# All loads of an attention opening issued at once, its value products grouped by tile shape over two banks, its weights later

## The chip, the cores and the metric

The kernel runs on one core of a Trainium2 chip. The metric is the device time of one execution in microseconds (us), the median of several runs of the same built program. Instructions run on five engines: TensorE (PE, with its weight loads shown apart as PEld), VectorE (DVE), ScalarE (ACT), GpSimd (POOL) and SyncE (SP), which issues the DMAs here. Matmuls write PSUM, which has eight banks of 2 KB in each partition; ACT and DVE read it from there.

## The reference

Retention attention without softmax, then a feed-forward layer with a softplus between its two matrices:

```python
scores = scale * np.matmul(q, k.transpose(0, 1, 3, 2))      # 8 batches, 8 heads, 576 x 576, head size 64
ret = scores * Dmat[None, :, :, :]                          # gamma_h ** (i - j) for i >= j, else 0
x = np.matmul(ret, v)                                       # -> 4608 tokens x 512
h = x @ w_in                                                # 512 x 2048
g = np.maximum(h, 0.0) + np.log1p(np.exp(-np.abs(h)))
return (g @ w_out).astype(np.float32)                       # 2048 x 512
```

All inputs and the output are float32.

## The kernel before

**Tiles.** The 4608 tokens are cut into 36 chunks of 128 (`C`), and four chunks make a unit of 512 tokens (nine units). The attention is computed chunk by chunk with a running state of 64 x 64 for each head: a chunk's scores within itself, and a cross term from the state of the chunks before it. The feed-forward layer goes by slots: slot `i` takes unit `i // 16` and block `p = i % 16` of 128 hidden columns. `hidden_mm(i)` is 12 matmuls of 128x512 (L380), `logs` (L388 to L390, ACT) and `softplus` (L394, DVE) follow, `softplus_split` writes the tile `g` (L398 ACT, L399 DVE), and `output_mm(i)` is again 12 matmuls (L412), issued one slot later. Each feed-forward operand is split into a high and a low part, so three products stand for one.

**The first nine chunks** go by doubles. Double `m` is chunk `m // 2` with two pairs of heads, 18 doubles in all, from float32 operands that DMA brings as one block of 512 KB each (`load_double`). For one double:
- `scale_next` (L138, POOL) scales its queries, `scale_values` (L154, ACT, four instructions) its values;
- `scores_double` (PE) makes four score products (L162: 64 rows by 128 columns of the array) and, where a later chunk follows, four state products (L167: 128 rows by 64 columns), into two PSUM banks;
- `scores_double_out`: DVE masks the scores (L177, two instructions) and adds up the state (L186, or a copy at L188), POOL scales the state (L190);
- `values_double` (PE) makes four products of values and masked scores (L203: 128 rows by 64 columns) and, from double 2 on, four cross products of the state and the queries (L207: 64 rows by 64 columns) that add to the same sums. Before, the two pairs (`s`) take turns: two L203, two L207, two L203, two L207, all into one bank;
- `values_double_out`: ACT copies the sums into the unit's tile `xt` as the high part (L216) and DVE takes the rest (L217).

**The opening** handles doubles 0 to 8 (`AHEAD` is 9) before the first slot: doubles 0 to 7 are all of unit 0. In iteration `m`, PE gets the scores of double `m` and then the values of double `m - 1` (at `m = 8` the values come first). It also prepares the first weights. A weight piece is 512 KB of a 64-bit float's two halves; `load_weight` brings it, `weight_a` (ACT L444, DVE L446), `weight_b` (DVE L452), `weight_c` (ACT L460) and `weight_d` (DVE L465) turn it into a high and a low part. Pieces `2p` and `2p + 1` belong to block `p`. Three staging buffers (`WBUFS`) hold pieces, so piece `n` is loaded after `weight_d(n - 3)`.

**Slots 0 to 18** run the feed-forward of unit 0 (and the first slots of unit 1). The odd ones of them, 1 to 17, each hold one of doubles 9 to 17 (scores of `m`, values of `m - 1`), with two banks for both; slot 18 holds the values of double 17. Slots 0 to 14 also prepare two weight pieces each. From slot 19 on, other code with smaller loads makes the attention; the change leaves it alone.

**What sets the order.** The order of each engine is the order of the code, which is written out by hand; nothing is scheduled anew. Five matmuls of 128x256 on a constant (`OPENING`, L498) run while the first loads are under way. All loads and weight loads stand in one queue, SP's, in which a load that waits for its buffer holds back those behind it.

Of the kernel before, what the change touches and what calls it, by code (L numbers as in the profile page):

```python
# [7 lines left out]
F32 = mybir.dt.float32  # L8
# [11 lines left out]
P = 128  # L20
# [14 lines left out]
NPLAIN = PCHUNK * NPAIR  # L35
LEAD = NPLAIN - 2 * (NDOUBLE - AHEAD) - 1
PIECE = 512
START_WEIGHTS = 3
OPENING = 5
OPEN = (6 * C + H + NPAIR, 6 * C)  # L40
RAWS = 2
WBUFS = 3
# [17 lines left out]
def retention_softplus_ffn(ctx: ExitStack, tc, opening, first, others, w, dec, vsc, gchp, out):  # L60
# [1 line left out]

    const = ctx.enter_context(tc.tile_pool(name="const", bufs=1))
    wpool = ctx.enter_context(tc.tile_pool(name="wpool", bufs=1))
    xpool = ctx.enter_context(tc.tile_pool(name="xpool", bufs=2))
    att = ctx.enter_context(tc.tile_pool(name="att", bufs=2))
    moe = ctx.enter_context(tc.tile_pool(name="moe", bufs=2))

# [3 lines left out]
    ps_h = ctx.enter_context(tc.tile_pool(name="ps_h", bufs=2, space=PSUM, side="right"))  # L72


    plain_pools, weight_pools = ExitStack(), ExitStack()
# [23 lines left out]

    def x_tile(u):  # L100
        if u not in xts:
            xts[u] = xpool.tile([P, 2, NKT, T], F32R, tag="xt", name=f"xt{u}")
        return xts[u]


# [1 line left out]
    def load_double(m):  # L107

        if m == 0:
            at = 0  # L110
            for x in parts:
                nc.sync.dma_start(x, opening[:, at:at + x.shape[1]])
                at += x.shape[1]
            kq, kv = (x[:, 0:4 * C] for x in parts)
        elif m == 5:
            kq, kv = (moe.tile([P, 4 * C], F32, tag="ab", name="raw_ab") for _ in range(2))
            for i, x in enumerate((kq, kv)):
                nc.sync.dma_start(x, first[m - 1][:, 4 * C * i:4 * C * (i + 1)])
# [74 lines left out]
    def values_double(m, bank):  # L193
# [17 lines left out]
    def values_double_out(m):  # L211
# [272 lines left out]

    next_double = [6]

    def load_next():
        if next_double[0] < NDOUBLE:
# [1 line left out]
            next_double[0] += 1  # L490

    def bank():
        return ps_att.tile([P, 4 * C], F32, tag="bank", name="bank")


    idle = ps_h.tile([P, T], F32, tag="h", name="idle")
    for n in range(OPENING):
        nc.tensor.matmul(idle[:, 0:2 * C], fill[:, 0:P], fill[:, 0:2 * C], start=True, stop=True)  # L498
    scale_next()
    scale_next()  # L500
    scale_values(0)
    for m in range(AHEAD):
        pair = [ps_y.tile([P, 4 * C], F32, tag=f"y{2 * (m % 2) + h}", name="pair") for h in range(2)]
        if m < AHEAD - 1:
            scores_double(m, pair)
        if m > 0:
            values_double(m - 1, bank())
# [9 lines left out]
        if m in (2, 4, 7):  # L517
            weight_b(m // 2 - 1)
        if m in (3, 5):
            weight_d((m - 3) // 2)  # L520
        if 0 < m < AHEAD - 1:
            values_double_out(m - 1)
        if m in (2, 4, 7):
            weight_c(m // 2 - 1)
        if m in (1, 3, 6):
            weight_a(m // 3)
        scale_next()
    weight_d(START_WEIGHTS - 1)


    SPLIT = NPLAIN - LEAD
    for i in range(NSLOT):
        j = i + LEAD
        if i < SPLIT:
            m = AHEAD + (i - 1) // 2
            if i % 2:
                banks = [bank() for _ in range(2)]
# [3 lines left out]
                values_double_out(m - 1)  # L541
                if i > 1:
                    load_next()
                scale_next()
                if "raw" in later:
                    load_upto(NPLAIN + 1)
            elif i == SPLIT - 1:
                values_double(m, bank())
                values_double_out(m)
            n = START_WEIGHTS + 2 * i  # L550
            weight_a(n)
            weight_cd(n - 1)
# [123 lines left out]
```

## Time and profile before

| what | value |
|---|---|
| median of 3 runs | 954.53 us (954.09 to 954.82) |
| the profiled execution | 954.1 us, of which its span is 952.4 us |
| PE busy | 943.4 us, 99% of the span |
| DVE, ACT, POOL busy | 70%, 71%, 29% of the span |
| granted TensorE clock, mean | 0.999 of full speed |
| all waits of PE for another engine | 4.6 us: 1.5, 1.3, 0.8, 0.8, 0.2 |
| first hidden product starts | 25.81 us |
| DMA in the first 60 us | 14.04 MB, mean 234 GB/s |

The span runs from the first to the last instruction; the profiled execution's own time is 1.7 us more. Times in the rows count from the span's start. The busy time of an engine is its instructions' time; pipelined matmuls overlap, so for PE the starts of consecutive groups tell more than durations. A row of the timeline merges equal neighbours: start, time until the last of them ends, engine, line, operation, output and inputs with shapes, count, and in brackets the idle time before it and what ended that. A float32 matmul shows as two records, so four matmuls are "x8".

### The profile page before, as it was taken

To read this page: it belongs to the slowest core of one execution; us is meant where nothing else is said; L and a number is where in the kernel's file an instruction comes from. 1 tells how busy PE (TensorE), PEld (TensorE's weight loads), DVE (VectorE), ACT (ScalarE), POOL (GpSimd) and SP (SyncE) were. 2 spreads that over 40 slices of the span, in tenths; PEclk is the share of its full clock that TensorE was granted. 3 is DMA by queue.
4 is the path that set the end of the run, shared out by engine and by line. 5 is a ranking of instruction groups with operands and counts; after the bars stand their busy time and mean duration, and the time that the engine had idled before them with its cause. 6 is when DMAs were issued, how large, how long until landed. Compare 5 with 4: busy or idle time off the path is not lost.

```text
span 952.4 us, 14525 instructions
## 1 busy us (share of the span) xinstructions
PE 943.4 (99%) x4946; PEld 788.2 (83%) x4946; DVE 664.5 (70%) x1507; ACT 677.3 (71%) x1449; POOL 279.4 (29%) x497
## 2 busy tenths in 40 slices
PE   8999999999999999999999999999999999999998
PEld 5777778888888888888888888888888888888886
DVE  6788855777877777777777777777777777753222
ACT  6677756777777777777777777777777777764444
POOL 5111112333343332343343343233333333310000
PEclk9999999999999999999999999999999999999999
DMA  8566631212312132212212222213212222201001
GB/s 299 182 200 211 187 137 52 66 52 67 106 56 67 56 105 67 67 51 97 79 52 67 63 99 67 67 50 112 67 50 67 67 95 67 67 1 45 1 1 44
DMA packets 28729, 79.85 MB, mean 84 GB/s; under 512 B 3440, under 2 KB 3440, under 8 KB 28656
## 3 DMA queue, kind: packets, MB, share of 16 engines
q1 hardware_dynamic: 28656, 78.93, 25.7%
q8 instruction: 39, 0.64, 0.3%
q14 instruction: 34, 0.28, 0.1%
HBM read 69.48 MB, written 9.44 MB: 83 GB/s over the span
## 4 chain that ended last, share of the span: by engine, by line
PE 97%; DMA 1%; ACT 1%; DVE 0%; SPq 0%; issue 0%; POOL 0%; ACTq 0%; DVEq 0%
PE h L380 41%; PE y L412 41%; PE os L348 6%; PE sc L266 3%; PE os L275 2%; PE bank L207 1%; PE bank L203 1%; DMA raw_g<-first 1%; PE bank L162 1%; PE pair L162 0%; PE pair L167 0%; PE bank L167 0%; DVE ab L394 0%; DVE g L399 0%; ACT ab L390 0%
## 5 line engine op out<-in xcount | busy, mean ns | idle before, releaser
L380 PE MATMUL h<-xt,w 128*128 128x512 f32 (+1 forms) x1740 | 419.6, 390 | 0.8 <-DVE w L465 0.8
L412 PE MATMUL y<-w,g 128*128 128x512 f32 x1728 | 415.1, 389 | 0.2 <-DVE g L399 0.2
L412 PEld LDWEIGHTS y<-w,g 128*128 128x128 f32 x1728 | 324.2, 188 | 67.9 <-DVE g L399 0.6
L380 PEld LDWEIGHTS h<-xt,w 128*128 128x128 f32 x1740 | 317.3, 188 | 63.0 <-DVE w L465 1.2
L241 POOL TENSOR_TENSOR raw<-raw,dec_sb 128x256 f32<-128x256 f32 x108 | 100.9, 934 | 425.5 <-DMA raw<-others 386.5
L399 DVE TENSOR_TENSOR g<-ab,g 128x512 fp32r<-128x512 f32 (+1 forms) x145 | 103.4, 713 | 87.4 <-ACT g L398 85.6
L394 DVE SCALAR_TENSOR_TENSOR ab<-h,ab 128x512 f32<-128x512 f32 (+1 forms) x145 | 99.7, 688 | 91.2 <-ACT ab L390 88.6
L398 ACT CAST g<-ab 128x512 fp32r<-128x512 f32 (+1 forms) x145 | 89.6, 618 | 99.0 <-DVE ab L394 97.8
L388 ACT ACTIVATE ab<-h 128x512 f32<-128x512 f32 (+1 forms) x145 | 86.3, 595 | 73.7 <-PE h L380 73.6
L390 ACT ACTIVATE ab<-ab 128x512 f32<-128x512 f32 (+1 forms) x145 | 91.3, 629 | 4.7
L389 ACT ACTIVATE ab<-ab 128x512 f32<-128x512 f32 (+1 forms) x145 | 91.3, 629 | 4.6
L255 ACT CAST hl<-raw 128x768 fp32r<-128x768 f32 x108 | 90.9, 841 | 0.0
L285 DVE TENSOR_TENSOR a<-sc,a 128x256 f32<-128x256 f32 x108 | 45.9, 425 | 60.9 <-ACT a L284 60.8
L361 ACT CAST xt<-os 64x128 fp32r<-64x128 f32 x216 | 56.4, 261 | 44.0 <-PE os L275 39.9
L257 DVE TENSOR_TENSOR hl<-raw,hl 128x512 fp32r<-128x512 f32 x108 | 84.7, 785 | 1.5
L348 PE MATMUL os<-ah,hl 128*128 128x256 f32 x324 | 72.7, 285 | 0.0
L365 DVE TENSOR_TENSOR xt<-os,xt 64x128 fp32r<-64x128 f32 x216 | 62.3, 288 | 2.8
L309 POOL TENSOR_TENSOR s<-s,gchp_sb 128x128 f32<-128x128 f32 x96 | 59.4, 618 | 10.5 <-DVE s L308 0.4
L348 PEld LDWEIGHTS os<-ah,hl 128*128 128x128 f32 x324 | 53.3, 191 | 0.1
L286 POOL TENSOR_SCALAR_AFFINE_SELECT a<-a 128x256 f32<-128x256 f32 x108 | 44.2, 410 | 29.6 <-DVE a L285 28.1
L256 DVE TENSOR_TENSOR hl<-raw,hl 64x256 fp32r<-64x256 f32 x108 | 45.9, 425 | 6.7 <-ACT hl L255 3.7
L317 ACT CAST ah<-a 128x256 fp32r<-128x256 f32 x108 | 44.0, 408 | 6.9 <-POOL a L286 3.9
(91 smaller groups left out, 782.5 us busy)
## 6 DMA issues: line engine op xcount, KB each, us to landing
raw<-others SPq DMA_DIRECT2D x108, 384.0 KB, 3.0
wst<-w SPq DMA_DIRECT2D x32, 512.0 KB, 3.7
out<-osb SPq DMA_DIRECT2D x34, 256.0 KB, 2.3
raw_rawp<-first SPq DMA_DIRECT2D x13, 512.0 KB, 4.9
raw_g<-first SPq DMA_DIRECT2D x3, 512.0 KB, 7.6
raw_ab<-first SPq DMA_DIRECT2D x2, 256.0 KB, 8.6
dec_sb<-dec SPq DMA_DIRECT2D x1, 512.0 KB, 3.6
out<-part SPq DMA_DIRECT2D x2, 256.0 KB, 2.4
```

Source lines behind the costliest of these rows:

```text
L241: nc.gpsimd.tensor_mul(r[:, 2:4], r[:, 2:4], later["dec"][:, 2 * pr:2 * pr + 2])
L255: nc.scalar.copy(hl[:, 0:6], r)
L257: nc.vector.tensor_sub(hl[:, 6:10], r[:, 2:6], hl[:, 2:6].bitcast(F32))
L348: nc.tensor.matmul(o[:, :, 0:width], lhs, rhs, start=(n == 0), stop=(n == len(mms) - 1))
L380: nc.tensor.matmul(h, ws[p][:, a, kt * P:(kt + 1) * P], xt[:, b, kt, cols], start=(n == 0), stop=(n == 3 * NKT - 1))
L388: nc.scalar.activation(ab, h, AF.Abs)
L389: nc.scalar.activation(ab, ab, AF.Exp, scale=-1.0)
L390: nc.scalar.activation(ab, ab, AF.Ln, bias=1.0)
L394: nc.vector.scalar_tensor_tensor(ab, h, 0.0, ab, op0=ALU.max, op1=ALU.add)
L398: nc.scalar.copy(g[:, HI], ab)
L399: nc.vector.tensor_sub(g[:, LO], ab, g[:, HI].bitcast(F32))
L412: nc.tensor.matmul(y, g[:, a, at:at + P], ws[p][:, b, PIECE:], start=(p == 0 and n == 0), stop=(p == NF - 1 and n == 2))
```

## The change

1. **Value products.** `values_double` now makes all four L203 products (L202 now) and then all four L207 products (L208 now). The two pairs write two different banks, at columns 384 to 511 of each. `ps_att` becomes one tile of two banks instead of two tiles of one. In the opening the odd iterations use the two `ps_h` banks instead, and there the copy out takes two instructions of 128 columns on ACT and two on DVE. Elsewhere one instruction on each reads both banks. In the odd slots the tile of two banks holds the scores and state products of double `m` too. In the built program ACT's copy there now waits for DVE's state sum, the third of DVE's reads of that tile; before, it waited for the second mask product only.
2. **Loads.** All nine loads of the opening are issued at its start. Doubles 5 to 8 go into four buffers of a new pool `rawx`, whose room is the odd units' `xt` buffer, opened in slot 1 (`xodd`) when these doubles are done; `xpool` keeps one buffer, for the even units. Load 3 now stands ahead of the first weight piece.
3. **Weights.** Pieces 0, 1, 2 are loaded after loads 3, 5, 7 and their steps come one to two iterations later; `weight_b(2)` comes after the opening, and `weight_c(2)`, `weight_d(2)` in slot 0.
4. **Warm-up.** Four matmuls at the start, and one after the scores of double 0, instead of five.

```diff
-OPENING = 5
+VCOLS = slice(3 * C, 4 * C)
+OPENING = (4, 1)
-    xpool = ctx.enter_context(tc.tile_pool(name="xpool", bufs=2))
+    xpool = ctx.enter_context(tc.tile_pool(name="xpool", bufs=1))
-    ps_att = plain_pools.enter_context(tc.tile_pool(name="ps_att", bufs=2, space=PSUM))
+    ps_att = plain_pools.enter_context(tc.tile_pool(name="ps_att", bufs=1, space=PSUM))
-    wst = weight_pools.enter_context(tc.tile_pool(name="wst", bufs=WBUFS, side="right"))
+    wst = weight_pools.enter_context(tc.tile_pool(name="wst", bufs=WBUFS))
+    rawx = load_pools.enter_context(tc.tile_pool(name="rawx", bufs=4, side="right"))
...
-            pool, tag = (moe, "g") if m in (3, 4, 8) else (rawp, "rawp")
+            pool, tag = (moe, "g") if m in (3, 4) else (rawx, "rawx") if 4 < m < AHEAD else (rawp, "rawp")
...
-        o = bank[:, 2 * C:4 * C].rearrange("p (s c) -> p s c", s=2)
+        o = [b[:, VCOLS] for b in banks]
         for s in range(2):
             for h in range(2):
                 rows = slice(h * D, (h + 1) * D)
-                nc.tensor.matmul(o[rows, s], L["v"][:, s, rows], L["a"][:, h, s], start=True,
+                nc.tensor.matmul(o[s][rows], L["v"][:, s, rows], L["a"][:, h, s], start=True,
                                  stop=not n_cross, skip_group_check=True)
-            for h in range(2) if n_cross else ():
-                rows = slice(h * D, (h + 1) * D)
-                nc.tensor.matmul(o[rows, s, 0:n_cross], L["before"][rows, s], L["q"][rows, s, 0:n_cross],
-                                 start=False, stop=True, skip_group_check=True)
+        if n_cross:
+            for s in range(2):
+                for h in range(2):
+                    rows = slice(h * D, (h + 1) * D)
+                    nc.tensor.matmul(o[s][rows, 0:n_cross], L["before"][rows, s], L["q"][rows, s, 0:n_cross],
+                                     start=False, stop=True, skip_group_check=True)
...
-        nc.scalar.copy(xt[:, HI, pr:pr + 2, cols], o)
-        nc.vector.tensor_sub(xt[:, LO, pr:pr + 2, cols], o, xt[:, HI, pr:pr + 2, cols].bitcast(F32))
+        if both is None:
+            parts = [(pr + s, o[s]) for s in range(2)]
+        else:
+            parts = [(slice(pr, pr + 2), both[:, :, VCOLS])]
+        for p, src in parts:
+            nc.scalar.copy(xt[:, HI, p, cols], src)
+        for p, src in parts:
+            nc.vector.tensor_sub(xt[:, LO, p, cols], src, xt[:, HI, p, cols].bitcast(F32))
...
-    for m in range(6):
+    for m in range(AHEAD):
         load_double(m)
-        if m in (2, 5):
-            load_weight(m // 3)
+        if m in (3, 5, 7):
+            load_weight((m - 3) // 2)
...
-        if m in (2, 3, 4, 7, 8):
+        if m in (3, 6):
             load_next()
-        if m in (3, 5, 7):
-            load_weight((m + 1) // 2)
+        if m in (5, 8):
+            load_weight(m // 3 + 2)
...
-    weight_d(START_WEIGHTS - 1)
+    weight_b(START_WEIGHTS - 1)
...
-                banks = [bank() for _ in range(2)]
-                scores_double(m, banks)
-                values_double(m - 1, banks[1])
+                both = bank()
+                scores_double(m, halves(both))
+                values_double(m - 1, halves(both))
+                if "xodd" not in later:
+                    load_pools.close()
+                    later["xodd"] = ctx.enter_context(tc.tile_pool(name="xodd", bufs=1, side="right"))
                 scores_double_out(m)
-                values_double_out(m - 1)
+                values_double_out(m - 1, both)
```

PE in the opening, iterations 4 and 5 (`pair` are score banks, `a_260` the masked scores of double 3, `s_192` the state), before:

```order
L162 MATMUL pair<-raw_g 128x128 x4
L167 MATMUL pair<-raw_g 64x64 x4
L203 MATMUL bank<-a_260,raw_g 64x128 x2
L207 MATMUL bank<-raw_g,s_192 64x128 x2
L203 MATMUL bank<-a_260,raw_g 64x128 x2
L207 MATMUL bank<-raw_g,s_192 64x128 x2
L162 MATMUL pair<-raw_ab 128x128 x4
```

The same place in the changed program:

```order
L165 MATMUL pair<-raw_g 64x64 x4
L202 MATMUL bank<-a_267,raw_g 64x128 x4
L208 MATMUL bank<-raw_g,s_202 64x128 x4
L160 MATMUL pair<-raw_rawx 128x128 x4
L165 MATMUL pair<-raw_rawx 64x64 x4
L202 MATMUL hv<-a_303,raw_g 64x128 x4
L208 MATMUL hv<-raw_g,s_233 64x128 x4
```

The two shapes of the value products follow each other once in a double instead of three times; every second double writes the `ps_h` banks (`hv`).

SP's queue from its start (`part` is double 0, `wst` a weight piece, the others doubles in order), before:

```order
L112 DMA part_93<-opening 128x780
L112 DMA part_94<-opening 128x768
L122 DMA raw_rawp<-first 128x1024 x2
L438 DMA wst<-w 128x1024
L122 DMA raw_g<-first 128x1024 x2
L118 DMA raw_ab<-first 128x512 x2
L438 DMA wst<-w 128x1024
L122 DMA raw_rawp<-first 128x1024 x2
L438 DMA wst<-w 128x1024
```

And in the changed program:

```order
L114 DMA part_96<-opening 128x780
L114 DMA part_97<-opening 128x768
L120 DMA raw_rawp<-first 128x1024 x2
L120 DMA raw_g<-first 128x1024
L446 DMA wst<-w 128x1024
L120 DMA raw_g<-first 128x1024
L120 DMA raw_rawx<-first 128x1024
L446 DMA wst<-w 128x1024
L120 DMA raw_rawx<-first 128x1024 x2
L446 DMA wst<-w 128x1024
L120 DMA raw_rawx<-first 128x1024
```

Load 3 (the first `raw_g`) has moved ahead of weight piece 0, and loads 6 to 8 up from the middle of the opening; none of these rows waits for a buffer any more.

## Rows read from the trace of the kernel before

**Rows 1.** The page's part 1: busy time, share of the span, instructions, by engine.

```profile
PE 943.4 (99%) x4946; PEld 788.2 (83%) x4946; DVE 664.5 (70%) x1507; ACT 677.3 (71%) x1449; POOL 279.4 (29%) x497
```

**Rows 2.** The view of waits, PE, whole span: us in total, times, longest.

```profile
PE pair L162 <- POOL raw_rawp L138: 1.3, 1, 1.3
PE h L380 <- DVE w L465: 0.8, 1, 0.8
PE pair L162 <- POOL raw_g L138: 0.8, 1, 0.8
PE y L412 <- DVE g L399: 0.2, 1, 0.2
```

**Rows 3.** Timeline of the opening, loads and PE: start, us, engine, line, operation.

```profile
1.53 3.92 PE L498 MATMUL idle<-fill 128*128 128x256 f32 x10 [1.53 <-DVE fill L474]
...
6.90 1.06 ACT L154 ACTIVATE raw_rawp<-raw_rawp,part 128x64 f32<-128x64 f32 x4 [0.81 <-DMA raw_rawp<-first]
...
10.00 0.40 POOL L190 TENSOR_TENSOR s<-s,part 128x128 f32<-128x128 f32 x1 [1.04 <-DVE s L188]
...
10.75 1.06 ACT L154 ACTIVATE raw_g<-raw_g,part 128x64 f32<-128x64 f32 x4 [0.41 <-DMA raw_g<-first]
...
11.57 0.71 PE L162 MATMUL pair<-raw_g 64*128 64x128 f32 x8 [0.77 <-POOL raw_g L138]
```

**Rows 4.** Timeline of the opening, PE's value products of doubles 0 and 3.

```profile
8.72 0.61 PE L203 MATMUL bank<-a,part 128*64 128x128 f32 x8
...
9.26 0.72 PE L162 MATMUL pair<-raw_rawp 64*128 64x128 f32 x8
...
14.85 0.39 PE L203 MATMUL bank<-a,raw_g 128*64 128x128 f32 x4
...
15.17 0.44 PE L207 MATMUL bank<-raw_g,s 64*64 64x128 f32 x4
...
15.53 0.44 PE L203 MATMUL bank<-a,raw_g 128*64 128x128 f32 x4
...
15.90 0.44 PE L207 MATMUL bank<-raw_g,s 64*64 64x128 f32 x4
...
16.27 0.71 PE L162 MATMUL pair<-raw_ab 64*128 64x128 f32 x8
```

**Rows 5.** Timeline of slots 0 to 2, PE.

```profile
25.81 3.04 PE L380 MATMUL h<-xt,w 128*128 128x512 f32 x12
...
37.54 3.06 PE L380 MATMUL h<-xt,w 128*128 128x512 f32 x12 [0.79 <-DVE w L465]
...
40.80 3.04 PE L412 MATMUL y<-w,g 128*128 128x512 f32 x12 [0.20 <-DVE g L399]
```

**Rows 6.** Timeline of slot 0, DVE.

```profile
27.42 0.42 DVE L446 TENSOR_SCALAR wst<-wst 128x512 int32<-128x512 uint32 x1
...
27.95 1.04 DVE L452 SCALAR_TENSOR_TENSOR wst<-wst 128x512 int32<-128x512 int32 x1
...
30.90 0.69 DVE L394 SCALAR_TENSOR_TENSOR ab<-h,ab 128x512 f32<-128x512 f32 x1 [1.91 <-ACT ab L390]
```

**Rows 7.** Timeline of slots 5 and 7, PE, first score product of each.

```profile
57.03 0.71 PE L162 MATMUL bank<-raw_rawp 64*128 64x128 f32 x8
...
70.49 0.72 PE L162 MATMUL bank<-raw_rawp 64*128 64x128 f32 x8
```

**Rows 8.** Timeline, DVE, the tile g of slots 1, 3 and 13.

```profile
40.05 0.69 DVE L399 TENSOR_TENSOR g<-ab,g 128x512 fp32r<-128x512 f32 x1
...
53.12 0.68 DVE L399 TENSOR_TENSOR g<-ab,g 128x512 fp32r<-128x512 f32 x1
...
119.97 0.69 DVE L399 TENSOR_TENSOR g<-ab,g 128x512 fp32r<-128x512 f32 x1
```

**Rows 9.** Timeline of slot 5, DVE's state sum and ACT's copy.

```profile
61.27 0.28 DVE L186 TENSOR_TENSOR s<-bank,s 128x128 f32<-128x128 f32 x1
...
61.38 0.37 ACT L216 CAST xt<-bank 128x256 fp32r<-128x256 f32 x1 [1.98 <-DVE a L177]
```

More of the change, by code (lines that the diff above doesn't have):

```diff
@@ L72, in retention_softplus_ffn @@
     ps_h = ctx.enter_context(tc.tile_pool(name="ps_h", bufs=2, space=PSUM, side="right"))
-    plain_pools, weight_pools = ExitStack(), ExitStack()
-    ps_att = plain_pools.enter_context(tc.tile_pool(name="ps_att", bufs=2, space=PSUM))
+    plain_pools, weight_pools, load_pools = ExitStack(), ExitStack(), ExitStack()
+    ps_att = plain_pools.enter_context(tc.tile_pool(name="ps_att", bufs=1, space=PSUM))
     rawp = plain_pools.enter_context(tc.tile_pool(name="rawp", bufs=2))
     pconst = plain_pools.enter_context(tc.tile_pool(name="pconst", bufs=1))
-    wst = weight_pools.enter_context(tc.tile_pool(name="wst", bufs=WBUFS, side="right"))
+    wst = weight_pools.enter_context(tc.tile_pool(name="wst", bufs=WBUFS))
+    rawx = load_pools.enter_context(tc.tile_pool(name="rawx", bufs=4, side="right"))
     later = {}
@@ L101, in x_tile @@
         if u not in xts:
-            xts[u] = xpool.tile([P, 2, NKT, T], F32R, tag="xt", name=f"xt{u}")
+            xts[u] = later.get("xodd" if u % 2 else "", xpool).tile([P, 2, NKT, T], F32R, tag="xt", name=f"xt{u}")
         return xts[u]
@@ L114, in load_double @@
             kq, kv = (x[:, 0:4 * C] for x in parts)
[L115 to L118, printed above, removed]
         else:
-            pool, tag = (moe, "g") if m in (3, 4, 8) else (rawp, "rawp")
+            pool, tag = (moe, "g") if m in (3, 4) else (rawx, "rawx") if 4 < m < AHEAD else (rawp, "rawp")
             r = pool.tile([P, 8 * C], F32, tag=tag, name=f"raw_{tag}")
@@ L191, in scores_double_out, with values_double @@
             states[m % 2] = s
-    def values_double(m, bank):
+    def values_double(m, banks):
         L = live[-1 - m]
@@ L202, in values_double, with values_double_out @@
                 rows = slice(h * D, (h + 1) * D)
-                nc.tensor.matmul(o[rows, s], L["v"][:, s, rows], L["a"][:, h, s], start=True,
+                nc.tensor.matmul(o[s][rows], L["v"][:, s, rows], L["a"][:, h, s], start=True,
                                  stop=not n_cross, skip_group_check=True)
-            for h in range(2) if n_cross else ():
-                rows = slice(h * D, (h + 1) * D)
-                nc.tensor.matmul(o[rows, s, 0:n_cross], L["before"][rows, s], L["q"][rows, s, 0:n_cross],
-                                 start=False, stop=True, skip_group_check=True)
+        if n_cross:
[4 more added lines that the diff above has]
+                                     start=False, stop=True, skip_group_check=True)
         L["o"] = o
-    def values_double_out(m):
+    def values_double_out(m, both=None):
         o = live.pop(-1 - m)["o"]
@@ L483, in retention_softplus_ffn @@
     nc.gpsimd.memset(mask2[0:S % C, S % C:C], 0.0)
-    next_double = [6]
+    next_double = [AHEAD]
     def load_next():
@@ L492, in bank, with halves, warm @@
     def bank():
-        return ps_att.tile([P, 4 * C], F32, tag="bank", name="bank")
+        return ps_att.tile([P, 2, 4 * C], F32, tag="bank", name="bank")
+    def halves(tile):
+        return [tile[:, n] for n in range(2)]
     idle = ps_h.tile([P, T], F32, tag="h", name="idle")
-    for n in range(OPENING):
-        nc.tensor.matmul(idle[:, 0:2 * C], fill[:, 0:P], fill[:, 0:2 * C], start=True, stop=True)
+    def warm(count):
+        for n in range(count):
+            nc.tensor.matmul(idle[:, 0:2 * C], fill[:, 0:P], fill[:, 0:2 * C], start=True, stop=True)
+    warm(OPENING[0])
     scale_next()
@@ L503, in retention_softplus_ffn @@
         pair = [ps_y.tile([P, 4 * C], F32, tag=f"y{2 * (m % 2) + h}", name="pair") for h in range(2)]
+        if m % 2:
+            both, vbanks = None, [ps_h.tile([P, 4 * C], F32, tag="h", name="hv") for _ in range(2)]
+        else:
+            both = bank() if m else None
+            vbanks = m and halves(both)
         if m < AHEAD - 1:
             scores_double(m, pair)
+        if m == 0:
+            warm(OPENING[1])
         if m > 0:
-            values_double(m - 1, bank())
+            values_double(m - 1, vbanks)
         if m == AHEAD - 1:
             scores_double(m, pair)
-            values_double_out(m - 1)
-        if m in (2, 3, 4, 7, 8):
+            values_double_out(m - 1, both)
+        if m in (3, 6):
             load_next()
-        if m in (3, 5, 7):
-            load_weight((m + 1) // 2)
+        if m in (5, 8):
+            load_weight(m // 3 + 2)
         scale_values(m + 1)
         scores_double_out(m)
[L517 to L520, printed above, removed]
+        if m in (3, 6):
+            weight_b(m // 3 - 1)
+        if m in (4, 7):
+            weight_d(m // 3 - 1)
         if 0 < m < AHEAD - 1:
[L522 to L525, printed above, removed]
+            values_double_out(m - 1, both)
+        if m in (3, 6):
+            weight_c(m // 3 - 1)
+        if m in (2, 5, 8):
             weight_a(m // 3)
         scale_next()
-    weight_d(START_WEIGHTS - 1)
+    weight_b(START_WEIGHTS - 1)
     SPLIT = NPLAIN - LEAD
@@ L536, in retention_softplus_ffn @@
             if i % 2:
-                banks = [bank() for _ in range(2)]
-                scores_double(m, banks)
-                values_double(m - 1, banks[1])
+                both = bank()
[4 more added lines that the diff above has]
+                    later["xodd"] = ctx.enter_context(tc.tile_pool(name="xodd", bufs=1, side="right"))
                 scores_double_out(m)
-                values_double_out(m - 1)
+                values_double_out(m - 1, both)
                 if i > 1:
@@ L547, in retention_softplus_ffn @@
             elif i == SPLIT - 1:
-                values_double(m, bank())
-                values_double_out(m)
+                both = bank()
+                values_double(m, halves(both))
+                values_double_out(m, both)
             n = START_WEIGHTS + 2 * i
```

## The prediction, made before the changed kernel ran

> **What bounds the kernel now.** I start with the page's busy times: PE is busy for 99% of the span [rows 1], so a gain has to be less work on PE or one of its few waits. The view of waits names them [rows 2]: besides the wait for the warm-up's constant they sum to 3.1 us, all of it in the first 41 us, and behind that PE never stands. So whatever shortens PE's row of work behind 41 us arrives at the end in full, unless another engine becomes the bound. For that I read the timeline, first PE in the opening [rows 3, 4], then PE, DVE and ACT in the slots [rows 5 to 9]. The reader is to see two things there. PE loses time where the shapes of its products change. And from slot 1 to slot 13 DVE and ACT, which prepare weights there, are nearly as slow as PE: DVE finishes `g` of slot 1 at 40.74 and PE starts to use it at 40.80, having stood for it; `g` of slot 3 ends 13.06 us later, while PE needs 13.46 from one odd slot to the next [rows 5, 7, 8].
>
> **The value products.** Where all four products of one shape stand together they take 0.54 us (8.72 to 9.26). The first two of them take 0.32 where a change of shape follows (14.85 to 15.17), so two more in the same shape cost 0.22. In turns, each further group of two takes 0.36 or 0.37 (15.17 to 15.53, to 15.90, to 16.27). Double 3 takes 1.42 so; grouped it should take 0.54 for the first shape and 0.36 + 0.22 for the second, 1.12 [rows 4]. That is 0.30 less for each double with a cross term: 2 to 17, sixteen. The cross products of doubles 8 and 9 are half as wide, but the cost is the change, so I take 0.30 there too. The second bank has no row of its own: between 0 (a new bank costs as much as a new shape) and 0.30 I take 0.30, since the four score products also alternate between two banks and run at the steady pace.
>
> **The opening.** Everything up to the values of double 1 stays, since it hangs on the first three loads, whose order stays. The shorter warm-up, four products of 3.92 / 5 = 0.78 each, lets double 0 start up to 0.4 us earlier, but double 1 then waits for load 1 as before (1.3 us of waits), so it is worth nothing [rows 2, 3]. Load 3 is next. Load 2, weight piece 0 and load 3 land in the 3.85 us between ACT's first use of load 1 and of load 3, 1.28 each; without piece 0 ahead of it load 3 lands near 9.45 instead of 10.7. But POOL works on double 1's state until 10.40, and from there the scaling and its hand-over to PE take the 0.8 that lie between load 3's use at 10.75 and PE's start at 11.57, so PE starts double 3 at 11.2: 0.37 of the 0.77 us wait [rows 3]. Bounds: 0, if POOL is late, and 0.77. Then come six value groups, doubles 2 to 7, of 0.30: 1.8. Against it stands DVE, which gets more work in a shorter stretch (the odd iterations' copies in two parts, weight steps later); I take 0.1 for the last masked scores coming late, between 0 and 0.5. Sum of the opening: 0.37 + 1.8 - 0.1 = 2.1 us, bounds 1.3 and 2.6; the first hidden product starts near 23.7 instead of 25.81 [rows 5].
>
> Covers in the opening. The loads: at 1.28 each behind load 1 at 6.87, load 4 lands at 12.0 and is scaled at 12.8, PE wants it at 13.25; loads 5 to 8 land at 13.3, 15.8, 17.1, 19.7, PE wants them at 15.3, 17.35, 19.4 and 22.6. Load 4 has the least slack, 0.45; each further us of lateness would be a us lost. On SP, pieces 0 to 2 move behind loads 3, 5 and 7, and loads 9 and 10 and pieces 3 and 4 follow; piece 3 is the twelfth block behind load 1, 6.87 + 12 x 1.28 = 22.2, and is wanted when slot 0 begins. A copy of 128 columns has no row; two of them cost between one and two of the 0.37 us that 256 columns take [rows 9], on ACT and likewise on DVE. The last copy before the first hidden product is a single one, so I price this at nothing beyond the 0.1 above.
>
> **Slots 0 to 2.** DVE gets `weight_a(2)` and `weight_b(2)` into the stretch before slot 0's softplus; it idles 1.91 us there, and the two are 0.42 and at most 1.04 [rows 6], so they are covered, by 0.4 at the worst. From the first hidden product to the output product of slot 1 pass 14.99 us (25.81 to 40.80), of which PE stands 0.99 for DVE [rows 5]: the chain of logs, softplus, weights and `g` sets this stretch, not PE. So double 8's 0.30 is lost here. And the chain grows: ACT's copy, so far released by DVE's second mask product, has to wait for the state sum too. In slot 5 that ends at 61.55, the copy began at 61.38 [rows 9], and ACT works without a pause behind it. That adds 0.2 us. Slots 0 to 2: +0.2, between -0.3 and +0.4.
>
> **Slots 3 to 13**, six pairs of slots. PE's pair falls from 13.46 [rows 7] to 13.16. The chain took 13.06 in the first pair, where PE had just stood for it, and (120.66 - 40.74) / 6 = 13.32 on average, part of which is DVE and ACT waiting for PE [rows 8]. With the copy's 0.2 that is 13.26 to 13.52. I take 13.27, because the first pair is the one in which PE was held by the chain, as it will be in all. So each pair gains 0.19, not 0.30: six give 1.1. Bounds: 1.8 gained, if PE stays the bound, and 0.4 lost, at 13.52.
>
> Here a rule counts against the change. The row shows ACT's copy of value sums standing 1.98 us for a DVE instruction that reads other columns of the same bank [rows 9]. The Trainium skill (PSUM — Partial Sum Buffer, "PSUM bank collisions raise a hardware error") says that two engines must not touch one bank in the same partitions at once, reads against reads included. By that rule a copy that reads both banks has to stand behind all of DVE's reads of both, the state sum among them, and the trace agrees as far as it shows such a wait for the one bank. Without it the pairs would come out at PE's 13.16.
>
> **Slots 14 to 18.** Weight preparation is over at slot 14, and nothing but PE binds: the values of doubles 15, 16 and 17 give 3 x 0.30 = 0.9.
>
> **Sum.** -2.1 + 0.2 - 1.1 - 0.9 = -3.9 us against the profiled execution's 954.1: 950.2. That execution was 0.4 us under the median of the runs, 954.53, so I forecast 950.6 for the median.
>
> **Rivals.** (a) The chain of DVE and ACT binds all the way, at 13.52 for a pair: for it, the average of 13.32 and the new wait; against it, the first pair's 13.06. Then -2.1 + 0.2 + 0.4 - 0.9 = -2.4, 952.1. (b) PE stays the bound: the copy's longer wait falls into time that DVE and ACT have, for instance because POOL's work, earlier by then, disturbs DVE less. Then -2.2 - 1.8 - 0.9 = -4.9, 949.6. (c) The change doesn't do what it says: with two banks the changes of shape cost what they did. Then the 0.37 of load 3 and the copy's 0.2 remain, 954.4; the 0.54 of a group of four speaks against it. (d) Slower: with 13 transfers outstanding the early loads share the engines with the later ones. Eleven blocks, loads 1 to 8 and pieces 0 to 2, at 1.28 would all land near 6.87 + 10 x 1.28 = 19.7, and PE's double 1 would start some 12.8 us late; less the 3.9 gained that is +8.9, 963.4. It decides as soon as load 1 lands more than 3.9 + 1.9 us later than 6.87. Against it: before, ten transfers are outstanding by then and still land one behind the other [rows 3].
>
> **How the numbers follow.** My forecast 0.49, (a) 0.22, (b) 0.20, (c) 0.06, (d) 0.03. A measurement of this kernel tells 0.2%, 1.9 us, from no change. The forecast, (b) and most of (a) are faster by more than that, 0.87; (c) and (a)'s worst are within it, 0.09; (d) and whatever of (c) also loses are slower, 0.04. All gains at their bounds give -2.6 - 0.3 - 1.8 - 0.9 = -5.6, all losses -1.3 + 0.4 + 0.4 - 0.9 = -1.4. With the 0.4 that is 948.9 to 953.1; both ends at once are rare on the upper side, so I cut it to 952.9, and that leaves out about 2 in 10 with (c) and (d).
>
> **What would show it.** First hidden product between 23.2 and 24.5; a value group of 1.12 us; a wait of at most 0.4 for load 3; the output product of slot 1 near 38.9; waits of PE for `g`, some 0.1 us each, in the even slots up to 14, with ACT's copies released by DVE's state sum; no wait of PE behind slot 14. It is wrong if the value group stays above 1.3, if the first hidden product comes after 25, or if an odd pair takes more than 13.5 us.

## The result and the profile after

The changed kernel takes 956.29 us (median of 14 runs, 955.67 to 958.20), the kernel before 954.24 beside it (14 runs): a ratio of 1.0022, with an interval of 1.0015 to 1.0030. It is 2.0 us slower, not 3.9 faster, and lies above the forecast's range. The profiled execution has a span of 954.4 us.

Most of what the prediction named is there all the same. The page's first part and the waits of PE, to be held against [rows 1, 2]:

```profile
span 954.4 us, 14523 instructions
PE 946.1 (99%) x4946; PEld 789.2 (83%) x4946; DVE 662.2 (69%) x1511; ACT 676.3 (71%) x1453; POOL 276.5 (29%) x497
```

```profile
PE h L388 <- DVE w L473: 1.0, 1, 1.0
PE pair L160 <- POOL raw_rawx L136: 0.8, 1, 0.8
PE pair L160 <- POOL raw_rawp L136: 0.2, 1, 0.2
PE y L420 <- DVE g L407: 0.2, 1, 0.2
```

The waits fell from 3.1 to 2.2 us, yet PE is busy for 2.7 us more with the same 4,946 instructions. That is the first sign: the loss is no wait, the same products take longer. Next the opening, of the changed kernel, by the timeline (load 3 is the first `raw_g`, load 6 the second `raw_rawx`), against [rows 3, 4]:

```profile
10.71 0.72 PE L160 MATMUL pair<-raw_g 64*128 64x128 f32 x8
...
13.72 0.61 PE L202 MATMUL bank<-a,raw_g 128*64 128x128 f32 x8
...
14.26 0.65 PE L208 MATMUL bank<-raw_g,s 64*64 64x128 f32 x8
...
14.85 0.72 PE L160 MATMUL pair<-raw_rawx 64*128 64x128 f32 x8
...
16.97 1.06 ACT L152 ACTIVATE raw_rawx<-raw_rawx,part 128x64 f32<-128x64 f32 x4 [1.57 <-DMA raw_rawx<-first]
...
17.80 0.71 PE L160 MATMUL pair<-raw_rawx 64*128 64x128 f32 x8 [0.83 <-POOL raw_rawx L136]
```

A value group takes 1.13 us (13.72 to 14.85) where it took 1.42, and load 3 holds nothing up any more. New is a wait of 0.83 for load 6. The first hidden product and the slots, against [rows 5, 7]:

```profile
24.09 3.06 PE L388 MATMUL h<-xt,w 128*128 128x512 f32 x12
...
38.90 3.02 PE L420 MATMUL y<-w,g 128*128 128x512 f32 x12 [0.18 <-DVE g L407]
...
49.37 3.06 PE L388 MATMUL h<-xt,w 128*128 128x512 f32 x12
52.57 3.06 PE L420 MATMUL y<-w,g 128*128 128x512 f32 x12
55.56 0.72 PE L160 MATMUL bank<-raw_rawp 64*128 64x128 f32 x8
...
68.82 0.72 PE L160 MATMUL bank<-raw_rawp 64*128 64x128 f32 x8
...
82.08 0.72 PE L160 MATMUL bank<-raw_rawp 64*128 64x128 f32 x8
```

A pair of slots takes 13.26 us (55.56 to 68.82 to 82.08) where it took 13.46. The starts of products in the timeline, from here to the end, tell where the time goes:

| product | before | changed | difference |
|---|---|---|---|
| hidden, slot 0 | 25.81 | 24.09 | -1.72 |
| output of slot 1 | 40.80 | 38.90 | -1.90 |
| output of slot 13 | 121.49 | 119.23 | -2.26 |
| hidden, slot 19 (unit 1) | 152.82 | 150.03 | -2.79 |
| hidden, slot 32 (unit 2 begins) | 236.88 | 235.13 | -1.75 |
| slot 48 (unit 3) | 341.36 | 339.61 | -1.75 |
| slot 64 (unit 4) | 444.08 | 443.61 | -0.47 |
| slot 80 (unit 5) | 548.55 | 548.09 | -0.46 |
| slot 96 (unit 6) | 651.28 | 652.09 | +0.81 |
| slot 112 (unit 7) | 755.76 | 756.57 | +0.81 |
| slot 128 (unit 8) | 857.88 | 859.98 | +2.10 |

2.8 us are gained up to slot 19. Then every odd unit loses 1.28 us (1.04 in the thirteen slots of unit 1 from slot 19 on) and no even unit loses anything: 0.080 us for each slot of an odd unit, 64 slots, 5.1 us. Two slots of unit 3, first of the kernel before, then of the changed one:

```profile
417.92 2.91 PE L380 MATMUL h<-xt,w 128*128 128x512 f32 x12
420.66 2.88 PE L412 MATMUL y<-w,g 128*128 128x512 f32 x12
...
424.45 2.91 PE L380 MATMUL h<-xt,w 128*128 128x512 f32 x12
```

```profile
417.13 2.96 PE L388 MATMUL h<-xt,w 128*128 128x512 f32 x12
419.94 2.90 PE L420 MATMUL y<-w,g 128*128 128x512 f32 x12
...
423.75 2.96 PE L388 MATMUL h<-xt,w 128*128 128x512 f32 x12
```

There is no wait in either. Twelve hidden products take 2.81 us from their start to the output's (417.13 to 419.94) where they took 2.74 (417.92 to 420.66). In unit 3 their mean spacing (from start to start) is 233.6 ns in the changed kernel and 229.2 before; in unit 4 it is 228.5 in both. The output products behind them in unit 3 are spaced 228.7 ns instead of 226.6, and 12 x (4.4 + 2.1) ns is the slot's 0.08 us. What differs between odd and even units is the tile `xt` alone: the change gave the odd units' tile another place. As built, the weights start at byte 16576 of each partition, the odd tile before at 164032, now at 212960.

### The profile page after: what moved, and what is told of

It is laid out like the page before. It is cut to its first block, busy times and chain, and to the rows that moved or that the text cites. A ratio compares the mean times of both kernels' runs of the same rounds, so it can differ in the third digit from the quotient of the medians.

```text
span 954.4 us, 14523 instructions
## 1 busy us (share of the span) xinstructions
PE 946.1 (99%) x4946; PEld 789.2 (83%) x4946; DVE 662.2 (69%) x1511; ACT 676.3 (71%) x1453; POOL 276.5 (29%) x497
## 4 chain that ended last, share of the span: by engine, by line
PE 96%; ACT 1%; DVE 1%; DMA 0%; POOL 0%; issue 0%; DVEq 0%; ACTq 0%; POOLq 0%
PE h L388 41%; PE y L420 40%; PE os L356 6%; PE sc L274 3%; PE os L283 2%; PE bank L208 1%; PE pair L160 1%; PE bank L202 1%; PE bank L160 0%; PE idle L511 0%; DMA wst<-w 0%; PE pair L165 0%; DVE a L175 0%; DVE ab L402 0%; DVE g L407 0%; ACT ab L397 0%
```

## The experiments

Each ratio is against the kernel before, measured beside that run on the same chip.

**1. The odd tile moved by 32 bytes.** The pools on the right side grow downward, so a tile of 32 unused bytes ahead of `rawx` moves the odd tile to 212928. Nothing is computed differently. (The buffers of the small loads lie below that tile and move too, but odd and even units use them alike.)

```diff
+    pad = ctx.enter_context(tc.tile_pool(name="pad", bufs=1, side="right"))
+    pad.tile([P, 8], F32, name="pad")
     plain_pools, weight_pools, load_pools = ExitStack(), ExitStack(), ExitStack()
```

> The changed kernel with an unused tile of 32 bytes ahead of the odd units' tile, which then starts at a multiple of 64 bytes (212928) instead of 32 past one (212960). The changed kernel loses 0.080 us in each of the 64 slots of units 1, 3, 5 and 7 and nothing in the even units. Theory A, the start of the tile within 64 bytes: the 64 slots take what they took before the change, so 956.3 - 64 x 0.080 = 951.2 us; the opening and slots 0 to 18 keep their gain of 2.8 us. Rival B, the place of the tile (near the top of SBUF, beside the buffers of the small loads): stays at 956.3.

Measured 951.37 us, ratio 0.9965 [0.9952, 0.9977]. Odd units' slots are again as long as before to the hundredth. Two slots of unit 3:

```profile
415.86 2.91 PE L390 MATMUL h<-xt,w 128*128 128x512 f32 x12
418.61 2.88 PE L422 MATMUL y<-w,g 128*128 128x512 f32 x12
...
422.40 2.91 PE L390 MATMUL h<-xt,w 128*128 128x512 f32 x12
```

So 32 bytes of address are worth about 5 us (4.9 by the two medians), and without that loss the change is 3 us faster than the kernel before.

**2. The odd tile moved by 64 bytes** (the same tile with 16 columns, address 212896).

> The same with 64 bytes: the odd units' tile moves further than in the other run, but starts 32 past a multiple of 64 again (212896). Theory A: 956.3 us, 0.080 us lost in each odd unit's slot. If a mere move mended it, it would come to 951.2 like the other, and A would fall.

Measured 954.78, ratio 1.0004 [0.9995, 1.0013]: odd slots are 0.053 us longer, not 0.080. It loses, as expected, but by a third less; "not a multiple of 64" has no room for two prices.

**3. The kernel before with its odd tile moved by 32 bytes** (the tile in a pool of its own between two unused tiles of 32 bytes; everything allocated behind it on the left side, `g` too, moves by 64).

> The kernel before, with only the odd units' tile moved by 32 bytes (164064 instead of 164032), everything behind it moved by 64. Theory A: each of the 64 slots of units 1, 3, 5 and 7 costs 0.080 us more, 954.2 + 5.1 = 959.3 us. Rival B: the place stays, so 954.2 us.

Measured 969.23, ratio 1.0150 [1.0135, 1.0166], 10 us more than expected. The loss is not in odd units alone. The page's groups of hidden (L385) and output (L417) products, then the same two of the kernel before:

```profile
L417 PE MATMUL y<-w,g 128*128 128x512 f32 x1728 | 426.3, 395 | 0.2 <-DVE g L404 0.2
L385 PE MATMUL h<-xt,w 128*128 128x512 f32 (+1 forms) x1740 | 424.4, 392 | 0.8 <-DVE w L470 0.8
```

```profile
L380 PE MATMUL h<-xt,w 128*128 128x512 f32 (+1 forms) x1740 | 419.6, 390 | 0.8 <-DVE w L465 0.8
L412 PE MATMUL y<-w,g 128*128 128x512 f32 x1728 | 415.1, 389 | 0.2 <-DVE g L399 0.2
```

The output products read `g` as weights and the tile `w` as moving rows, and neither is the odd tile; `g` had moved by 64 bytes, from one multiple of 64 to another, and they became 11.2 us slower. My theory of a multiple of 64 fell here. Every fast pair of tiles had one thing in common: the moving tile and the tile of weights start at the same place within 128 bytes. That gave two new theories for the next three runs: the distance between the two counts, or each must have its own place.

**4, 5 and 6. Distance or place.** 96 unused bytes on the right (odd tile at 212864); the same with 64 unused bytes ahead of everything on the left; and those 64 with the 32 of the first run.

```diff
     gchp_sb = const.tile([P, NPAIR], F32, name="gchp_sb")
+    const.tile([P, 16], F32, name="pad64")
```

> The change with 96 unused bytes ahead of the odd units' tile: it starts at 212864, a multiple of 128, while the weights, the even units' tile, g and hl all stay at addresses that leave 64 when divided by 128. Theory A (a matmul's moving rows must start at a multiple of 64): as with 32 unused bytes, 951.4 us, hidden products of odd units at 229 ns. Theory R (the moving rows and the weights loaded beside them must start at the same place within 128 bytes; the kernel before had all of them at 64): hidden products of odd units some 4 to 5 ns longer, 0.05 to 0.08 us more for each of 64 slots, 954.8 to 956.5. Theory S (each operand by itself must leave 64): as R here.

> As the kernel with the odd units' tile at a multiple of 128, and 64 more unused bytes ahead of everything on the other side, so that weights, both tiles, g and hl all start at multiples of 128. Theory A: 951.4 us. Theory R (the same place within 128 bytes is what counts): 951.4 us, every pitch as before. Theory S (each must leave 64): hidden and output products slow in every unit, 144 slots times some 0.16 us, near 974.

> 64 unused bytes ahead of weights, even units' tile, g and hl, which start at multiples of 128, and the odd units' tile left at 64 within 128 (the 32 byte pad). Theory A: 951.4 us. Theory R: hidden products of the odd units alone 4 to 5 ns longer, 954.8 to 956.5. Theory S: outputs slow in all units and hidden products in the even ones, 144 times 0.08 plus 80 times 0.08, near 969.

Measured, with the distance from the weights to the odd tile within 256 bytes as the programs were built:

| kernel | odd tile less weights | distance | odd slot | us | ratio |
|---|---|---|---|---|---|
| before | 147456 | 0 | 0 | 954.24 | 1 |
| 32 bytes of padding (run 1) | 196352 | 0 | 0.000 | 951.37 | 0.9965 [0.9952, 0.9977] |
| the change | 196384 | 32 | +0.080 | 956.29 | 1.0022 [1.0015, 1.0030] |
| 64 bytes (run 2) | 196320 | 224 | +0.053 | 954.78 | 1.0004 [0.9995, 1.0013] |
| run 4 | 196288 | 192 | +0.080 | 956.09 | 1.0019 [1.0010, 1.0028] |
| run 5 | 196224 | 128 | +0.067 | 955.42 | 1.0014 [1.0005, 1.0024] |
| run 6 | 196288 | 192 | +0.080 | 956.58 | 1.0026 [1.0016, 1.0035] |

Run 6 has the odd tile where run 1 had it and is slow; runs 4 and 6 have neither the weights nor the odd tile at the same address, but the same distance and the same price. So it is the distance. Run 5 was meant to be fast by a period of 128 and is not: the period that fits is 256. A period of 512 does not fit, since the distances of the kernel before and of run 1 differ by 191 x 256 bytes and both are fast.

**7. TensorE alone.** A kernel that leaves out the whole computation and makes stretches of 192 products, in the order of the hidden products, at nine distances. Beside TensorE only one copy of ACT's, 0.6 us, runs at the start of a stretch.

```diff
+    for xt in moving:
+        stretch(weights, xt)
+    stretch(weights, moving[0])
+    stretch(later_weights, moving[1])
+    stretch(later_weights, moving[0])
```

The tiles in `moving` start 0, 32, 64 and so on up to 256 bytes on from the weights, within 256; `later_weights` start 32 bytes on, so that the last but one stretch has both tiles moved by 32 and the last has a distance of 224.

> TensorE by itself: twelve stretches of 192 products (64 or fewer instructions of other engines run only before and after a stretch), each product with 128x128 weights and 512 moving columns in the order of the hidden products. The moving tile starts 0, 32, 64, 96, 128, 160, 192, 224 and 256 bytes past a multiple of 256 from the weights, then 0 again, then 0 with both moved by 32 bytes, then 224 with the weights moved. It leaves the whole computation out. Theory R256 (what counts is the distance between the two tiles that one product reads, within 256 bytes): about 227 ns per product (43.6 us a stretch) at 0, 256 and with both moved, 230 to 234 ns (44.3 to 44.9 us) at all others, as in the odd units of the runs with the tile moved (0.053 to 0.080 us in 12 products). Rival (the other engines' reads and writes collide with TensorE's, and TensorE alone does not care): 227 ns in all twelve.

The page's groups, named by the distance (busy us of a stretch, mean ns of a product's own duration):

```profile
L97 PE MATMUL h<-d_onesixty,weights 128*128 128x512 f32 x192 | 45.1, 396 | 0.0
L97 PE MATMUL h<-d_ninetysix,weights 128*128 128x512 f32 x192 | 45.0, 395 | 0.0
L97 PE MATMUL h<-d_thirtytwo,weights 128*128 128x512 f32 x192 | 45.0, 395 | 0.0
L97 PE MATMUL h<-d_oneninetytwo,weights 128*128 128x512 f32 x192 | 45.0, 394 | 0.0
L97 PE MATMUL h<-d_zero,weights_thirtytwo 128*128 128x512 f32 x192 | 45.0, 396 | 0.0
L97 PE MATMUL h<-d_onetwentyeight,weights 128*128 128x512 f32 x192 | 45.0, 395 | 0.0
L97 PE MATMUL h<-d_twotwentyfour,weights 128*128 128x512 f32 x192 | 45.0, 395 | 0.0
L97 PE MATMUL h<-d_sixtyfour,weights 128*128 128x512 f32 x192 | 44.1, 391 | 0.0
L97 PE MATMUL h<-d_thirtytwo,weights_thirtytwo 128*128 128x512 f32 x192 | 43.7, 389 | 0.0
L97 PE MATMUL h<-d_twofiftysix,weights 128*128 128x512 f32 x192 | 43.7, 389 | 0.0
```

At 256 and with both tiles moved by 32 a stretch takes 43.7 us, at every other distance but one 45.0 or 45.1: 1.3 / 192 = 6.8 ns for each product. Only 64 lies between, 44.1. (The two stretches at 0 stand in one group of 384 and are left out here: beside the first, ACT and DVE were still filling tiles. By the starts of its products the second has the pace of 256.) The granted clock was 1.00 in all eleven stretches behind the first. So no other engine is needed: the rival is out, and what counts is how TensorE's own two tiles lie to each other. How the two reads hinder each other no run here shows. The distance also explains run 3: there the moving `w` stands at a distance of 192 from `g`, its weights; 12 x 6.8 ns = 0.08 us in each of 144 slots is 11.7 us, where the group of output products had grown by 11.2.

One thing is left. Alone, the distances 32, 128, 192 and 224 cost the same, in the kernel between 0.053 and 0.080 us a slot. The starts of single products in unit 3 show why the two need not agree. In run 1 the first five hidden products behind the small products of the attention are spaced 228 to 236 ns, and only then 227, at which the output products go on. In the changed kernel the hidden products keep to 230 to 236 throughout, and the first five output products behind them are spaced 228 to 235, though their own two tiles have not moved against each other. It looks as if the run-up that run 1 pays on its hidden products falls on the output products there. In run 2 (224) these are spaced 227 from the second on, and that makes two thirds of what its slot loses less. Why they are spared the run-up is not shown.

**8. The change with the 32 bytes, its value products in the old order** (for each half two products on the scores, then two on the state).

> The change with the 32 byte pad (951.4 us), but the value products in the order of the kernel before: for each half the pair on the masked scores and then the pair on the state. Theory of the prediction (each group of 8 products costs 0.30 more in this order, on the chain of seven values in the opening, and on PE's row of the slots): H0 some 2.0 later, each pair of slots 3 to 13 longer by 0.1 to 0.3, slots 14 to 18 by up to 0.9: together 3.3 to 4.5 more, near 955. Rival (the order inside a group is worth nothing, the opening's gain is from the loads alone): 951.4, with H0 where it was.

Measured 954.16, ratio 0.9996 [0.9987, 1.0005], 2.8 us more than run 1, somewhat less than expected. The first hidden product starts at 25.38, only 0.43 ahead of before: that is what the loads bring without the grouping (the later weights and the split warm-up are in it too), beside the 0.37 I had put on load 3. A pair of slots is back at 13.45:

```profile
70.56 0.72 PE L162 MATMUL bank<-raw_rawp 64*128 64x128 f32 x8
...
84.01 0.71 PE L162 MATMUL bank<-raw_rawp 64*128 64x128 f32 x8
```

The 0.43 of the loads is gone again by the output of slot 13 (121.56 against 121.49). So without the grouping the other parts of the change bring nothing at the end. The grouping without the loads was not run.

**9. DVE's state sum behind ACT's copy in the odd slots**, with the 32 bytes.

```diff
-                scores_double_out(m)
-                values_double_out(m - 1, both)
+                scores_double_out(m, later_sum=True)
+                values_double_out(m - 1, both, lambda: state_double_out(m))
```

> The aligned version, and in the odd slots 1 to 17 DVE's state sum is issued behind ACT's copy, so that the copy waits for the two mask products alone, as before the change. Theory: DVE and ACT, not PE, set slots 1 to 13, and the copy's wait is 0.2 us of each pair of slots (13.38 us now); then the pairs come to 13.2 us and the run is 6 or 7 times 0.2 us = 1.2 to 1.4 us faster than the aligned version, near 950.0. Rival: the copy is not what lengthens the chain, or DVE pays for the sum where it now stands; then the same as the aligned version, 951.2.

Measured 950.08, ratio 0.9952 [0.9939, 0.9964], as expected, and 1.3 us under run 1, though the two intervals overlap. Slot 5, ACT's copy and DVE's sum of this kernel, to be held against [rows 9], and behind them the first score products of slots 7 and 9:

```profile
59.62 0.37 ACT L232 CAST xt<-bank 128x256 fp32r<-128x256 f32 x1 [2.02 <-DVE a L177]
...
60.10 0.29 DVE L193 TENSOR_TENSOR s<-bank,s 128x128 f32<-128x128 f32 x1 [0.56 <-ACT xt L232]
```

```profile
68.74 0.71 PE L162 MATMUL bank<-raw_rawp 64*128 64x128 f32 x8
...
81.90 0.72 PE L162 MATMUL bank<-raw_rawp 64*128 64x128 f32 x8
```

The copy no longer waits for the sum, and from slot 7 on a pair takes 13.16 us, what I had computed for PE alone. Where nothing else holds them up, pairs take 13.26 in the changed kernel and 13.29 to 13.33 in run 1, so the copy's wait costs 0.10 to 0.17 a pair. The first two pairs are no shorter: from the output product of slot 1 to those of slots 3 and 5 they take 13.79 and 13.75, in run 1 13.68 and 13.73. Not all of the 1.3 us is the copy's: in the two profiles the six pairs together differ by 0.80, and the opening, which the edit does not touch, ended 0.65 us later in run 1's (24.38 against 23.73).

**10. The second and third piece of weights asked for behind loads 6 and 8**, on top of run 9; the same kernel was run twice, and the rows are those of the second time.

```diff
-        if m in (3, 5, 7):
-            load_weight((m - 3) // 2)
+        if m in (3, 6, 8):
+            load_weight(m // 3 - (m < 8))
```

> The version with the 32 byte pad and the state sum behind the copy (950.1 us), with the second piece of weights asked for behind load 6 and the third behind load 8, not behind 5 and 7. Theory (load 6, whose landing at 16.97 held back TensorE by 0.8 in the change's profile, comes one load of 512 KB sooner, some 1.3 us): H0 up to 0.8 sooner, 949.3 to 950.1. Rival (the second weights, later by the same 1.3, now hold ScalarE back in the opening, with the copies and the values behind it): H0 0 to 0.7 later, 950.1 to 950.8.

> The same kernel as with the second and third piece of weights asked for behind loads 6 and 8, once more, for a profile at the full clock (the one taken with it had a granted clock of 0.85 and says nothing). Theory (it is no slower than 950.1 us, and TensorE has no wait for load 6 any more): 949.3 to 950.1, H0 23.3 to 23.9. Rival (the weights held back cost the opening as much as load 6 did): 950.1 to 950.8, H0 23.7 or later.

Measured 949.60, ratio 0.9946 [0.9933, 0.9960], and 949.83, 0.9953 [0.9941, 0.9966]. PE has no wait for load 6, and the first hidden product starts at 23.69, as in run 9 (23.73), whose profile had none either. So the 0.83 us in the changed kernel's profile is a load that lands late in some executions. It need not be load 6: in run 1, with the same opening, PE stands 1.53 us for load 1 and not at all for load 6. The intervals of runs 9 and 10 overlap: whether this order gains anything is open. 949.6 to 950.1 is where the best versions lie, 0.5% under the kernel before.

**11. Doubles loaded behind the slot's weights**, on top of run 10 (`load_next` and `scale_next` behind `weight_cd` in odd slots).

> As that kernel, but in the odd slots the load and the scaling of the next double are issued behind the weights of the slot, so that one piece of weights no longer queues behind 512 KB of the double. Theory (slots 4 to 7 lost their 0.3 to 0.6 us each, g(3) and g(5) late against the hidden products, to pieces of weights that land late): the weights land up to 1.3 us sooner in slots 3 to 7, 0.4 to 1.0 off the end, 948.6 to 949.2. Rival (those pieces are late because their buffer comes free late, in slot 1, where no double is loaded): no change, 949.4 to 949.8.

Measured 950.54, ratio 0.9964 [0.9951, 0.9978]: not faster than run 10, and whether it is slower is open, since the intervals overlap. The pieces of weights land no sooner against their use (ACT waits 0.55 and 0.92 us for those of slots 4 and 6, 0.49 and 0.76 in run 10), and the double comes late instead. Slot 7:

```profile
66.65 1.15 POOL L138 TENSOR_TENSOR raw_rawp<-raw_rawp,part 128x256 f32<-128x256 f32 x1 [6.35 <-DMA raw_rawp<-first]
...
67.85 0.71 PE L162 MATMUL bank<-raw_rawp 64*128 64x128 f32 x8 [0.32 <-POOL raw_rawp L138]
```

## Why the prediction was wrong

**The step that failed** is the sentence "whatever shortens PE's row of work behind 41 us arrives at the end in full, unless another engine becomes the bound". It took the length of a product for fixed. The change moves the odd units' tile, and I priced that move not at all. It costs 64 slots x 0.080 = 5.1 us (the output products' share included), because the new place stands 32 bytes, within 256, from the weights that are loaded beside it (shown by runs 1, 4, 5 and 6 in the kernel and by run 7 for TensorE alone). None of my rivals was this one; rival (d), the only slower one, did not occur. Once the distance is mended the sentence holds: in run 1's profile the hidden product of slot 19 starts 2.06 us ahead of before, and that of slot 128 still 2.05.

Without that loss the steps were right in kind, and their sum too large by 0.8: run 1 took 951.37, inside the range. By the starts in the table above, all from one profile:

- **Opening: forecast -2.1, measured -1.72.** The value group took 1.13 (forecast 1.12) and load 3's wait went as a whole. The step that was off is the cover of load 6, estimated to land at 15.8 and wanted at 17.35: ACT could use it only at 16.97, and PE stood for 0.83. That is this execution's: in the profiles of runs 1, 2, 4, 5, 6 and 9, whose opening is the same, load 6 holds nothing up, 0.33 or 0.34 is left of load 3's wait (forecast 0.40), and the first hidden product starts between 23.66 and 24.38, a gain of 1.43 to 2.15. Run 8 shows the parts: without the grouping only 0.43 is left.
- **Slots 0 to 2: forecast +0.2, measured -0.18**, within the bounds. PE stands 1.21 us there for DVE, 1.03 of it for `w`.
- **Slots 3 to 13: forecast -1.1, measured -0.36.** The pairs, from the output product of one odd slot to the next, took 13.67, 13.33, 13.26, 13.26, 13.49 and 13.32 against my 13.27. In the first, which is over the 13.5 that I had named as a sign of being wrong, the output product of slot 3 began 3.20 us after the hidden product ahead of it (49.37 to 52.57), not the 2.72 of slots 5, 7 and 9. The copy's wait is not the reason, since without it the first pair took 13.79 (run 9). The chain in front of it starts at a piece of weights that ACT waits for in slot 2, longer than before; the changed kernel first, then the kernel before:

```profile
39.85 0.69 ACT L452 ACTIVATE wst<-wst 128x512 f32<-128x512 f32 x1 [1.16 <-DMA wst<-w]
```

```profile
41.07 0.69 ACT L444 ACTIVATE wst<-wst 128x512 f32<-128x512 f32 x1 [0.47 <-DMA wst<-w]
```

  That this piece is the cause is read from the rows, not shown; run 11, which was to bring the later ones sooner, failed to and a fourth staging buffer was not tried.
- **The copy's wait, forecast 0.2 a pair**, is there. ACT's copy in slot 5 ends its idle time on DVE's state sum:

```profile
60.00 0.28 DVE L184 TENSOR_TENSOR s<-bank,s 128x128 f32<-128x128 f32 x1
...
60.37 0.37 ACT L223 CAST xt<-bank 128x256 fp32r<-128x256 f32 x1 [2.23 <-DVE s L184]
```

  Its price was half of that or a little more: in the steady pairs 13.26 with it (13.29 to 13.33 in run 1), 13.16 without (run 9). By the rule of the Trainium skill that the prediction weighed (PSUM — Partial Sum Buffer, "PSUM bank collisions raise a hardware error") one of the two has to stand behind the other; the trace agrees, since in run 9 it is the sum that waits 0.56 us for the copy. Which of them waits is the kernel's choice, and the sum's user is farther off.
- **Slots 14 to 18: forecast -0.9, measured -0.53** (-2.26 to -2.79). This has in it a loss of 0.24 by address in slots 16 to 18, which are of unit 1 already. In run 1 the stretches between the output products of slots 13, 15, 16 and 17, with one value group each, gain 0.21, 0.30 and 0.29, as forecast or a little less.

Most of what I gave as signs of being right appeared (24.09 for the first hidden product, 1.13 for the group, 38.90 for slot 1, no wait behind slot 14); of the waits for `g` the view lists only one, 0.18 in slot 2. These signs ended at slot 19, and a forecast whose gain is in the first 150 us should have named a sign in the other 800 as well: the mean time of the products there, which the page's two largest groups show.

## What to carry to other kernels

When a change moves a tile that TensorE reads, in a kernel that is bound by TensorE, work out the distance in bytes between the moving tile and the weights' tile before and after: with 32-bit operands and 512 columns a multiple of 256 ran at 226.7 ns a product, the other distances tried at 228.9 (64 bytes) to 234.3 (160). A pool on the other side of the memory, or an odd-sized constant ahead of it, changes it unseen, and a tile of a few unused bytes sets it right. When PE's busy time grows with the same instructions and no new waits, compare the mean time of the same group by unit before looking for a stall.

## What the runs showed that I had not expected

- TensorE's pace depends on the distance between the two tiles that it reads: 45.0 or 45.1 us for 192 products at six of the seven distances tried between 0 and 256 bytes, 44.1 at 64, 43.7 at a multiple of 256. The Trainium skill (SBUF — State Buffer, "Operand start alignment") asks for a start at a multiple of the element size and says that this is about legality, not speed; every address here keeps it, and the run times differ by up to 1.5%.
- A restart seems to cost more than the wait. In the changed kernel the output products of slot 5 start on time (63.18 to 65.90 is twelve hidden products at full pace) but run for 2.99 us, where those of slot 4 ran for 2.88:

```profile
60.46 2.88 PE L420 MATMUL y<-w,g 128*128 128x512 f32 x12
63.18 2.88 PE L388 MATMUL h<-xt,w 128*128 128x512 f32 x12
65.90 2.99 PE L420 MATMUL y<-w,g 128*128 128x512 f32 x12
```

  The second of them starts 286 ns after the first and the next nine are spaced 224 to 236, where those of slot 4 are spaced 225 to 228: much the run-up that stands behind the attention's small products in unit 3 of run 1, with no wait there. `g` of slot 5 is the tile that DVE finishes last before them, so I take the stream to be broken by a wait too short for the view to list; 0.11 us is about what a pair lost against run 9. That the break itself costs it was not tried apart.
